# Attention with beacon keys into a two-layer network: transposes moved from TensorE to DMA from the third batch on, and the first two batches reordered

## The chip, the cores and the metric

The kernel runs on one core of a Trainium2 chip. The metric is device time in microseconds (us), as the median of several runs of the whole program. A profile is one more execution, recorded by the hardware profiler; its span is the time from its first instruction to its last.

The core has five engines, each with its own queue of instructions that it takes in order: TensorE (PE in the profile; PEld is its weight load), VectorE (DVE), ScalarE (ACT), GpSimd (POOL) and SyncE (SP). SP does no arithmetic here: it issues DMAs. ScalarE and GpSimd issue DMAs as well, between their other work. An instruction that has to wait stops everything behind it in its engine's queue.

## The reference

Eight batches, eight heads, 576 queries and keys of width 64, and 16 extra "beacon" keys per head that every query sees:

```python
k_all = np.concatenate([beacon_k, k], axis=2)
v_all = np.concatenate([beacon_v, v], axis=2)
scores = scale * np.matmul(q, k_all.transpose(0, 1, 3, 2))
causal = np.zeros((S, Nb + S), dtype=bool)
causal[:, Nb:] = np.triu(np.ones((S, S), dtype=bool), k=1)
scores = np.where(causal, -1000000000.0, scores)
a = np.exp(scores - scores.max(-1, keepdims=True))
a /= a.sum(-1, keepdims=True) + 1e-09
attn_out = np.matmul(a, v_all)
x = attn_out.transpose(0, 2, 1, 3).reshape(B * S, H * D)   # 4608 x 512
h = x @ w_in                                               # 512 x 2048
out = np.maximum(0.01 * h, h) @ w_out                      # 2048 x 512
```

## The kernel before, in words

**Pairs and steps.** Attention is done by pairs of heads, numbered g = 0 to 31; a batch b has four pairs, hp = 0 to 3, so g = 4b + hp. The loop at the end of the kernel runs over g; I call one turn of it a step. A pair passes through three steps: in step g its scores and exponentials, in step g + 2 its values (`value`, two halves), in step g + 3 its output is transposed into `xT` (`finish`). The program order within each engine is the order in which the code writes the instructions (`manual_schedule`).

**Q and K.** `load_qk` (L137) loads two pairs of a batch (a "group", grp 0 or 1) by DMAs that GpSimd issues, into `q_raw` and `k_raw`. `permute` (L167), on GpSimd apart from the first tiles, copies them into `q_nat` and `k_nat`, 128 partitions by 9 blocks of 128. `t_q` (L229 to L252) transposes one pair: nine TensorE transposes of 64x128 into PSUM (tag `tp`), for Q and again for K, and a copy by VectorE into `qT` or `kT` that also puts the rows into order (L249). The transposed beacon keys (`bkT`) are copied into the first 16 columns of `kT` (L239).

**Scores and values.** `score(g, n)`, n = 0 to 3, multiplies into one of two PSUM buffers (pool `ps_sc`), and ScalarE takes the exponential out of it into `aT` (L278, L282). `masks` (L292 to L305, VectorE) zeroes the upper triangles. `value` multiplies `aT` with the values (tile `av` in PSUM); VectorE takes the reciprocal of the sums and writes `x_nat` (L342, L343). `x_transposes` (L355) transposes `x_nat` with five TensorE transposes, and VectorE copies into `xT` (L360).

**V.** `load_v` (L211, L214, L216) loads a batch's values by six DMAs that SP issues; `cast_v` (L225) turns them to bf16, on VectorE for batches 0 and 1, on GpSimd after that. The load of batch 2 (in `loads(3)`) is tied with `behind` to the last load of `w_out`, so that it starts only when the weights are there.

**The network as filler.** The second part is cut into 9 chunks of 512 tokens. `moe1` (L369) is four matmuls and a ScalarE activation into `gT` (L376); `moe2` (L385) is four matmuls, and after every fourth call a VectorE copy into `osb` (L394) and a store that SP issues (L396). `fill()` puts one of these calls where the step has a `slot`: none in steps 0 to 5, four in steps 6 and 7, eight from step 9 on, and a longer hand-written row of them in step 8, which also empties batch 1. A chunk can be filled only when `finish` of the last pair of its batch has raised `ready`.

**PSUM.** All of `tp`, `av` and `acc` (the filler's accumulator) take turns in one pool of four buffers, `ps_one`: the fifth tile waits until the first is read out.

**Loads in the loop.** `loads(g)` stands at the head of each step. For batches 1 to 6 it starts the next batch: values and Q/K loads at hp 0 and 1, `permute` at hp 2 and 3, `cast_v` at hp 3.

Of the kernel before, what the change touches and what calls it, by code (L numbers as in the profile page):

```python
# [15 lines left out]
def kernel(  # L16
# [24 lines left out]
    RI = 9  # L41
# [25 lines left out]

    singles = ctx.enter_context(tc.tile_pool(name="singles", bufs=1))
    rawpool = ctx.enter_context(tc.tile_pool(name="rawpool", bufs=2))
    qkpool = ctx.enter_context(tc.tile_pool(name="qkpool", bufs=4))  # L70
    natpool = ctx.enter_context(tc.tile_pool(name="natpool", bufs=3))
    headpool = ctx.enter_context(tc.tile_pool(name="headpool", bufs=2))
    gpool = ctx.enter_context(tc.tile_pool(name="gpool", bufs=2))
    opool = ctx.enter_context(tc.tile_pool(name="opool", bufs=3))
# [129 lines left out]
            reason="loads in order of need",  # L204
        )

    def load_v(b, after=None):

        t = rawpool.tile([128, NKB, H, D], FP32, name="v_raw")
        v_raws[b] = t  # L210
        first = nc.sync.dma_start(out=t[0:NB, 0], in_=beacon_v[b].rearrange("h p d -> p h d"))  # L211
        if after is not None:
            behind(first, after)
        nc.sync.dma_start(out=t[NB:128, 0], in_=v[b, :, 0:112].rearrange("h p d -> p h d"))  # L214
        for c in (1, 2, 3, 4):
            last = nc.sync.dma_start(  # L216
                out=t[0 : ROWS[c], c],
                in_=v[b, :, OFF[c] : OFF[c] + ROWS[c]].rearrange("h p d -> p h d"),
            )
        return last  # L220
# [8 lines left out]
    def t_q(g, which, copy=nc.vector.tensor_copy):  # L229

        b, hp = divmod(g, NPAIR)
        grp, e = divmod(hp, 2)
        ps_ = slice(e * RP, (e + 1) * RP)
        if which == 0:
            dst = headpool.tile([128, S], BF16, name="qT")
            qk[g] = [dst]
        else:
            kT = headpool.tile([128, NB + S], BF16, name="kT")
            nc.vector.tensor_copy(out=kT[:, 0:NB], in_=bkT[:, b, hp])  # L239
            qk[g].append(kT)  # L240
            dst = kT[:, NB : NB + S]
        ps = ps_one.tile([128, 1024], BF16, name="tp", tag="one")
        for i in range(RI):
            nc.tensor.transpose(  # L244
                ps[:, i * RP : (i + 1) * RP],
                nat[b, grp][which][ps_, i].rearrange("p h d -> p (h d)"),
                ident[ps_, ps_],
            )
        copy(  # L249
            out=dst.rearrange("c (p i) -> c p i", i=RI),  # L250
            in_=ps[:, 0:S].rearrange("c (i p) -> c p i", i=RI),
        )  # L252

    probs = {}

# [58 lines left out]
    def value(g, half):  # L314
        b, hp = divmod(g, NPAIR)
        aT = probs[g]
        va = v_bufs[b % 2]
        if half == 0:
            xs[g] = (
                headpool.tile([128, 5, 2, D], BF16, name="x_nat"),  # L320
                headpool.tile([128, 10], FP32, name="rec"),
            )
        x_nat, rec = xs[g]
        t0, t1 = ((0, 3), (3, 5))[half]
        av = ps_one.tile([128, 512], FP32, name="av", tag="one")
        avv = av[:, 0 : (t1 - t0) * 132].rearrange("p (n w) -> p n w", w=66)
        for t in range(t0, t1):
            q0, _ = QT[t]
            for par in range(2):
                n = (t - t0) * 2 + par  # L330
                for c in range(t + 1):
                    a0 = acol(c, q0)
                    nc.tensor.matmul(  # L333
                        out=avv[:, n, 0 : D + 1],
                        lhsT=aT[0 : ROWS[c], par, a0 : a0 + 128],
                        rhs=va[0 : ROWS[c], c, 2 * hp + par, :],
                        start=(c == 0),
                        stop=(c == t),
                        skip_group_check=True,
                    )  # L340
        n0, n1 = t0 * 2, t1 * 2
        nc.vector.reciprocal(out=rec[:, n0:n1], in_=avv[:, :, D])  # L342
        nc.vector.tensor_tensor(  # L343
            out=x_nat[:, t0:t1].rearrange("p t e d -> p (t e) d"),
            in0=avv[:, :, 0:D],
            in1=rec[:, n0:n1, None].to_broadcast([128, n1 - n0, D]),
            op=ALU.mult,
        )

    def x_transposes(g):  # L350
        b, hp = divmod(g, NPAIR)
        x_nat, _ = xs.pop(g)
        ps = ps_one.tile([128, 1024], BF16, name="tp", tag="one")
        for t, (q0, rows) in enumerate(QT):
            nc.tensor.transpose(  # L355
                ps[:, q0 : q0 + rows],
                x_nat[0:rows, t].rearrange("p e d -> p (e d)"),
                ident[0:rows, 0:rows],
            )
        nc.vector.tensor_copy(out=xT[:, hp, b * S : (b + 1) * S], in_=ps[:, 0:S])  # L360

    gT = {}

# [71 lines left out]
    with order:  # L435
# [24 lines left out]
        def loads(g):  # L460
            b, hp = divmod(g, NPAIR)
            if g == 1:
                for which in range(2):
                    permute(1, 0, which, nc.gpsimd.tensor_copy)
            elif g == 3:
                for which in range(2):
                    permute(1, 1, which, nc.gpsimd.tensor_copy)
                behind(load_w_in(0), v1)
                for i in range(1, 4):
                    load_w_in(i)  # L470
                for i in range(4):
                    w = load_w_out(i)
                load_v(2, after=w)
                load_qk(2, 0)
                load_qk(2, 1)
            elif b >= 1 and b < B - 1:
                if b > 1:
                    if hp == 0:
                        load_v(b + 1)
                    if hp < 2:  # L480
                        load_qk(b + 1, hp)
                if hp >= 2:
                    for which in range(2):
                        permute(b + 1, hp - 2, which, nc.gpsimd.tensor_copy)
                if hp == 3:
                    cast_v(b + 1, nc.gpsimd)

        def finish(g):

            x_transposes(g)  # L490
            b, hp = divmod(g, NPAIR)
            if hp == NPAIR - 1:
                ready[0] = NCH if b == B - 1 else b + 1


        for g in range(NG + 3):
            if has(g):
                loads(g)
            slots = [0] * 8 if g < 6 else [0, 0, 1, 1, 0, 1, 1, 0] if g < 8 else [1] * 8

            def slot(n):
                if slots[n]:
                    fill()

            if g == 2 * NPAIR:

                finish(g - 3)
                value(g - 2, 0)
                fill()
                value(g - 2, 1)  # L510
                fill()
                value(g - 1, 0)
                finish(g - 2)
                value(g - 1, 1)
                fill()
                fill()
                finish(g - 1)
                for n in range(16):
                    fill()
                t_q(g, 0)  # L520
                t_q(g, 1)
                fill()
                fill()
                score(g, 0)
                score(g, 1)
                fill()
                fill()
                fill()
                t_q(g + 1, 0)
                t_q(g + 1, 1)  # L530
                score(g, 2)
                score(g, 3)
                fill()
                fill()
                masks(g)
                fill()
                continue

            late = g - 2 == 2 * NPAIR - 1 or g - 2 == 2 * NPAIR - 2
            if has(g):  # L540
                score(g, 0)
                score(g, 1)
            slot(0)
            if g == 2:
                cast_v(0, nc.vector)
            if g == NPAIR + 1:
                cast_v(1, nc.vector)
            if has(g - 3) and not 2 * NPAIR < g <= 2 * NPAIR + 2:
                finish(g - 3)
            slot(1)  # L550
            if has(g - 2) and not late:
                value(g - 2, 0)
            slot(2)
            slot(3)
            if has(g + 1) and g + 1 != 2 * NPAIR:
                t_q(g + 1, 0)
                t_q(g + 1, 1)
            if has(g):
                score(g, 2)
                score(g, 3)  # L560
            slot(4)
            if has(g - 2) and not late:
                value(g - 2, 1)
            slot(5)
            if g == 2:
                beacon_transposes(1, B)
            slot(6)
            if has(g):
                masks(g)
            slot(7)  # L570
# [32 lines left out]
```

The softmax here doesn't subtract the row's maximum and nothing guards it: scores larger than these inputs give would overflow.

## Time and profile before

| | |
|---|---|
| median of 13 runs | 379.05 us (375.95 to 380.94) |
| the profiled execution | 380.18 us, its span 378.5 us |
| ScalarE busy | 195.5 us (52%) |
| VectorE busy | 173.6 us (46%) |
| GpSimd busy | 101.9 us (27%) |
| DMA traffic | 33.82 MB, mean 89 GB/s |
| score matmuls of pair 8 begin at | 77.98 us |

The first stage (steps 0 to 7, to about 55 us) has attention and hardly any filler, and its loads keep the DMA engines busy. The second stage is attention with the filler between; the last part, from about 312 us, is filler alone. "Idle before" in a line of the profile is the time that the engine stood still just ahead of these instructions, with what released it.

### The profile page before, as it was taken

What the parts mean: (1) busy time and instruction counts of PE and PEld (TensorE: products, weight loads), DVE (VectorE), ACT (ScalarE), POOL (GpSimd) and SP (SyncE); (2) the same over time, 40 slices, a digit from 0 to 9 for tenths busy, and PEclk for the clock granted to TensorE, in tenths of its full rate; (3) what the DMA queues carried; (4) which work ended last, traced back from release to release, by engine and by line L of the source; (5) the groups of instructions that cost most, each with busy time, mean ns of one, the idle gap of its engine ahead of it and who ended that gap; (6) DMA issues with size and microseconds to landing.
All of it is one profiled execution on the core that took longest, in us unless ns stands there. A gap on an engine that the chain in (4) does not pass through costs nothing.

```text
span 378.5 us, 7668 instructions
## 1 busy us (share of the span) xinstructions
PE 355.2 (94%) x3217; PEld 189.0 (50%) x3264; DVE 173.6 (46%) x402; ACT 195.5 (52%) x308; POOL 101.9 (27%) x143
## 2 busy tenths in 40 slices
PE   4878799999999899999999999999999999999996
PEld 3455455444555455545554555555555554444442
DVE  2669763063556664564456545644455233000021
ACT  3936585366536785347634873377336801643310
POOL 8479126657202822082018202300000000000000
PEclk9999899999999999999999999999999999999999
DMA  8898999946319930169014901100010002001012
GB/s 169 152 211 139 202 204 201 199 105 113 69 57 203 183 54 2 57 119 189 4 56 83 225 7 50 44 21 2 28 57 29 1 29 83 2 0 57 28 55 83
DMA packets 58370, 33.82 MB, mean 89 GB/s; under 512 B 41440, under 2 KB 53472, under 8 KB 58336
## 3 DMA queue, kind: packets, MB, share of 16 engines
q0 software_dynamic: 13152, 13.34, 22.5%
q1 hardware_dynamic: 44896, 19.67, 20.8%
q8 instruction: 25, 0.41, 0.4%
q10 hardware_dynamic: 288, 0.33, 0.3%
q14 instruction: 9, 0.07, 0.1%
HBM read 37.22 MB, written 9.44 MB: 123 GB/s over the span
## 4 chain that ended last, share of the span: by engine, by line
PE 84%; DVE 8%; DMA 3%; POOL 2%; issue 1%; SPq 1%; ACT 0%
PE acc L385 33%; PE acc L369 32%; PE av L333 7%; PE sc L267 6%; PE tp L244 4%; PE tp L355 2%; DMA v_raw<-in_v_dram 1%; DMA v_raw<-in_k_dram 1%; DVE osb L394 1%; DVE xT L360 1%; DVE x_nat L343 1%; SPq L216 1%; DVE qT L249 1%; DVE kT L249 1%; POOL k_raw L137 1%
## 5 line engine op out<-in xcount | busy, mean ns | idle before, releaser
L278 ACT ACTIVATE aT<-sc 128x928 bf16<-128x928 f32 (+2 forms) x128 | 102.5, 855 | 78.1 <-PE sc L267 77.9
L369 PE MATMUL acc<-xT,w_in_sb 128*128 128x512 bf16 x551 | 138.2, 380 | 3.6 <-DVE xT L360 2.1
L385 PE MATMUL acc<-w_out_sb,gT 128*128 128x512 bf16 x554 | 135.6, 379 | 1.5 <-issue 0.6
L376 ACT ACTIVATE gT<-acc 128x512 bf16<-128x512 f32 x144 | 85.6, 600 | 82.2 <-PE acc L369 81.0
L369 PEld LDWEIGHTS <-w_in_sb 128*128 128x128 bf16 x576 | 52.6, 98 | 60.0 <-issue 5.1
L385 PEld LDWEIGHTS <-gT 128*128 128x128 bf16 x576 | 52.1, 98 | 60.0 <-issue 5.3
L394 DVE COPY osb<-acc 128x512 f32<-128x512 f32 x36 | 24.8, 690 | 93.5 <-PE acc L385 93.0
L267 PE MATMUL sc<-qT,kT 64*128 64x128 bf16 (+5 forms) x384 | 43.1, 313 | 6.7 <-DVE kT L249 3.5
L333 PEld LDWEIGHTS <-aT 128*128 128x128 bf16 (+1 forms) x960 | 39.3, 101 | 16.4 <-issue 3.0
L333 PE MATMUL av<-v_aug,aT 128*128 128x65 bf16 (+1 forms) x960 | 42.5, 198 | 1.0 <-DVE xT L360 0.6
L167 POOL COPY q_nat<-q_raw 128x1152 bf16<-128x1152 bf16 (+1 forms) x16 | 18.3, 1145 | 85.7 <-PE tp L244 57.5
L249 DVE COPY qT<-tp 128x576 bf16<-128x576 bf16 x32 | 24.2, 755 | 34.4 <-PE tp L244 34.4
L343 DVE TENSOR_TENSOR x_nat<-av,rec 128x384 bf16<-128x384 f32 x64 | 31.4, 491 | 2.2
L267 PEld LDWEIGHTS <-kT 64*128 64x128 bf16 (+1 forms) x384 | 18.5, 101 | 20.9 <-issue 11.5
L225 POOL CAST v_aug<-v_raw 128x512 bf16<-128x512 f32 (+1 forms) x30 | 19.3, 683 | 33.2 <-PE av L333 31.5
L360 DVE COPY xT<-tp 128x576 bf16<-128x576 bf16 x32 | 14.5, 453 | 29.8 <-PE tp L355 29.8
L342 DVE RECIPROCAL rec<-av 128x6 f32<-128x6 f32 x64 | 11.9, 185 | 33.6 <-PE av L333 33.6
L137 POOL DMA_DIRECT2D k_raw<-in_k_dram x31 | 20.8, 671 | 9.8 <-DMA w_out_sb<-in_moe_w_out_dram 5.0
L249 DVE COPY kT<-tp 128x576 bf16<-128x576 bf16 x31 | 23.2, 748 | 0.0
L137 POOL DMA_DIRECT2D q_raw<-in_q_dram x31 | 19.5, 629 | 11.7 <-DMA v_raw<-in_v_dram 5.1
L299 DVE TENSOR_TENSOR aT<-aT,mask 128x768 bf16<-128x768 bf16 x32 | 21.6, 675 | 1.2 <-ACT aT L278 1.2
L167 POOL COPY k_nat<-k_raw 128x1152 bf16<-128x1152 bf16 (+1 forms) x16 | 18.7, 1171 | 0.6 <-DMA k_raw<-in_k_dram 0.6
(33 smaller groups left out, 150.3 us busy)
## 6 DMA issues: line engine op xcount, KB each, us to landing
out_dram<-osb SPq DMA_DIRECT2D x36, 256.0 KB, 2.0
v_raw<-in_v_dram SPq DMA_DIRECT2D x24, 256.0 KB, 6.0
q_raw<-in_q_dram POOLq DMA_DIRECT2D x31, 144.0 KB, 6.2
k_raw<-in_k_dram POOLq DMA_DIRECT2D x31, 144.0 KB, 6.5
w_in_sb<-in_moe_w_in_dram POOLq DMA_DIRECT2D x4, 512.0 KB, 8.1
w_out_sb<-in_moe_w_out_dram POOLq DMA_DIRECT2D x4, 512.0 KB, 16.7
v_raw<-in_v_dram SPq DMA_DIRECT2D x8, 224.0 KB, 4.8
v_raw<-in_v_dram SPq DMA_DIRECT2D x8, 160.0 KB, 5.3
```

Source lines behind the costliest of these rows:

```text
L137: dma = nc.gpsimd.dma_start(out=dst[e * RP : (e + 1) * RP], in_=src[b, h0 : h0 + 2].rearrange("h (p i) d -> p h i d", i=RI),)
L167: copy(out=dst[p0:p1], in_=src[p0:p1].rearrange("p h i d -> p i h d"))
L249: copy(out=dst.rearrange("c (p i) -> c p i", i=RI), in_=ps[:, 0:S].rearrange("c (i p) -> c p i", i=RI),)
L267: nc.tensor.matmul(out=sc[0 : ROWS[c], par, col - c0 : col - c0 + w], lhsT=kT[ps_, c * 128 : c * 128 + ROWS[c]], rhs=qT[ps_, q0 : q0 + w], ...
L278: last = nc.scalar.activation(out=aT[:, :, c0 : c0 + w], in_=sc[:, :, 0:w], func=AF.Exp, scale=0.125)
L299: nc.vector.tensor_tensor(out=diag, in0=diag, in1=tri[:, None, None, :].to_broadcast([128, 2, 3, 128]), op=ALU.mult,)
L333: nc.tensor.matmul(out=avv[:, n, 0 : D + 1], lhsT=aT[0 : ROWS[c], par, a0 : a0 + 128], rhs=va[0 : ROWS[c], c, 2 * hp + par, :], start=(c = ...
L343: nc.vector.tensor_tensor(out=x_nat[:, t0:t1].rearrange("p t e d -> p (t e) d"), in0=avv[:, :, 0:D], in1=rec[:, n0:n1, None].to_broadcast( ...
L369: nc.tensor.matmul(out=acc, lhsT=w_in_sb[:, j, fc * 128 : (fc + 1) * 128], rhs=xT[:, j, i * 512 : (i + 1) * 512], start=(j == 0), stop=(j ...
L376: nc.scalar.activation(out=gT[i][:, fc, :], in_=acc, func=AF.Prelu, alpha=0.01)
L385: nc.tensor.matmul(out=acc, lhsT=gT[i][:, fc, t * 128 : (t + 1) * 128], rhs=w_out_sb[:, fc, :], start=(fc == 0), stop=(fc == NF - 1),)
L394: nc.vector.tensor_copy(out=osb, in_=acc)
```

## The change

Two things are changed, and buffers with them.

First, steps 0 to 7 get an order of their own: the transposes of the next pair stand between the first two and the last two scores; in odd steps ScalarE copies K's transposes out of PSUM instead of VectorE; `finish` comes at the end of the step; the beacon keys' transposes and the two casts on VectorE move to other steps.

Second, from batch 2 on, Q and K are transposed by DMA (`turn_pairs`, two DMAs for a group of two pairs, issued by SP) and then put into order by VectorE from SBUF (`in_order`), a step ahead of use. The output of the first three pairs of each batch is transposed by DMA as well (`x_turn`, three DMAs issued by SP); the last pair of each batch keeps the TensorE transposes. The loads of the values of batches 3 to 7 are issued by ScalarE; that of batch 2 stays on SP. Step 8 has two `fill()` fewer.

```diff
-    qkpool = ctx.enter_context(tc.tile_pool(name="qkpool", bufs=4))
-    natpool = ctx.enter_context(tc.tile_pool(name="natpool", bufs=3))
+    qkpool = ctx.enter_context(tc.tile_pool(name="qkpool", bufs=3))
+    natpool = ctx.enter_context(tc.tile_pool(name="natpool", bufs=2))
+    turnpool = ctx.enter_context(tc.tile_pool(name="turnpool", bufs=2))
...
-    def load_v(b, after=None):
+    def load_v(b, after=None, queue=nc.sync):
...
+    turned = {}
+
+    def turn_pairs(b, grp):
+
+        tiles = []
+        for which, name in enumerate(("q_turn", "k_turn")):
+            t = turnpool.tile([128, RI, 2, RP], BF16, name=name)
+            nc.sync.dma_start_transpose(
+                out=t.rearrange("c i e p -> c i (e p)"),
+                in_=nat[b, grp][which].rearrange("r i h d -> r (i h d)"),
+            )
+            tiles.append(t)
+        turned[b, grp] = tiles
+
+    def in_order(g, eng):
+
+        b, hp = divmod(g, NPAIR)
+        grp, e = divmod(hp, 2)
+        qT = headpool.tile([128, S], BF16, name="qT")
+        kT = headpool.tile([128, NB + S], BF16, name="kT")
+        eng.tensor_copy(out=kT[:, 0:NB], in_=bkT[:, b, hp])
+        for t, dst in zip(turned[b, grp], (qT, kT[:, NB : NB + S])):
+            eng.tensor_copy(
+                out=dst.rearrange("c (p i) -> c p i", i=RI),
+                in_=t[:, :, e].rearrange("c i p -> c p i"),
+            )
+        qk[g] = [qT, kT]
...
-                headpool.tile([128, 5, 2, D], BF16, name="x_nat"),
+                headpool.tile([128, 5, 2, D], BF16, name="x_nat", bufs=3),
...
+    def x_turn(g):
+
+        b, hp = divmod(g, NPAIR)
+        x_nat, _ = xs.pop(g)
+        flat = x_nat.rearrange("p t e d -> p t (e d)")
+        dst = xT[:, hp, b * S : (b + 1) * S]
+        nc.sync.dma_start_transpose(out=dst[:, None, 0:112], in_=flat[0:112, 0])
+        nc.sync.dma_start_transpose(
+            out=dst[:, 112:496].rearrange("p (t q) -> p t q", t=3),
+            in_=flat[:, 1:4].rearrange("p t x -> p (t x)"),
+        )
+        nc.sync.dma_start_transpose(out=dst[:, None, 448:576], in_=flat[:, 4])
...
                 if b > 1:
                     if hp == 0:
-                        load_v(b + 1)
+                        load_v(b + 1, queue=nc.scalar)
                     if hp < 2:
                         load_qk(b + 1, hp)
                 if hp >= 2:
                     for which in range(2):
                         permute(b + 1, hp - 2, which, nc.gpsimd.tensor_copy)
+                    turn_pairs(b + 1, hp - 2)
                 if hp == 3:
                     cast_v(b + 1, nc.gpsimd)
+            if g + 1 >= 2 * NPAIR and has(g + 1):
+                in_order(g + 1, nc.vector)
 
         def finish(g):
 
-            x_transposes(g)
             b, hp = divmod(g, NPAIR)
+            if b < 2 or hp == NPAIR - 1:
+                x_transposes(g)
+            else:
+                x_turn(g)
...
                 for n in range(16):
                     fill()
-                t_q(g, 0)
-                t_q(g, 1)
-                fill()
-                fill()
                 score(g, 0)
                 score(g, 1)
                 fill()
                 fill()
                 fill()
-                t_q(g + 1, 0)
-                t_q(g + 1, 1)
                 score(g, 2)
                 score(g, 3)
...
+            if g < 2 * NPAIR:
+
+                score(g, 0)
+                score(g, 1)
+                if g == 3:
+                    beacon_transposes(1, B)
+                if g + 1 < 2 * NPAIR:
+                    t_q(g + 1, 0)
+                    t_q(g + 1, 1, nc.scalar.copy if g % 2 else nc.vector.tensor_copy)
+                slot(2)
+                if g != 2 and has(g - 2):
+                    value(g - 2, 0)
+                slot(3)
+                score(g, 2)
+                score(g, 3)
+                if g == 2:
+                    cast_v(0, nc.vector)
+                    value(0, 0)
+                slot(5)
+                if has(g - 2):
+                    value(g - 2, 1)
+                slot(6)
+                if g == NPAIR:
+                    cast_v(1, nc.vector)
+                if has(g - 3):
+                    finish(g - 3)
+                masks(g)
                 continue
```

The old places of `beacon_transposes(1, B)`, of the two casts and of `t_q(g + 1, ...)` in the general step are taken out. Steps from 9 on are otherwise as before.

More of the change, by code (lines that the diff above doesn't have):

```diff
@@ L205, in behind @@
         )
-    def load_v(b, after=None):
+    def load_v(b, after=None, queue=nc.sync):
         t = rawpool.tile([128, NKB, H, D], FP32, name="v_raw")
         v_raws[b] = t
-        first = nc.sync.dma_start(out=t[0:NB, 0], in_=beacon_v[b].rearrange("h p d -> p h d"))
+        first = queue.dma_start(out=t[0:NB, 0], in_=beacon_v[b].rearrange("h p d -> p h d"))
         if after is not None:
             behind(first, after)
-        nc.sync.dma_start(out=t[NB:128, 0], in_=v[b, :, 0:112].rearrange("h p d -> p h d"))
+        queue.dma_start(out=t[NB:128, 0], in_=v[b, :, 0:112].rearrange("h p d -> p h d"))
         for c in (1, 2, 3, 4):
-            last = nc.sync.dma_start(
+            last = queue.dma_start(
                 out=t[0 : ROWS[c], c],
@@ L537 @@
                 continue
+            if g < 2 * NPAIR:
[24 more added lines that the diff above has]
+                masks(g)
+                continue
             late = g - 2 == 2 * NPAIR - 1 or g - 2 == 2 * NPAIR - 2
@@ L543 @@
             slot(0)
[L544 to L547, printed above, removed]
             if has(g - 3) and not 2 * NPAIR < g <= 2 * NPAIR + 2:
@@ L554 @@
             slot(3)
-            if has(g + 1) and g + 1 != 2 * NPAIR:
-                t_q(g + 1, 0)
-                t_q(g + 1, 1)
             if has(g):
@@ L564 @@
             slot(5)
-            if g == 2:
-                beacon_transposes(1, B)
             slot(6)
```

## The prediction, made before the changed kernel was run

> **What bounds the kernel now.** I read the page's busy table first, then the timeline of TensorE in a steady group, then the timelines and waits of the engines that the change loads: SP's queue, ScalarE, VectorE.
>
> ```profile
> PE 355.2 (94%) x3217; PEld 189.0 (50%) x3264; DVE 173.6 (46%) x402; ACT 195.5 (52%) x308; POOL 101.9 (27%) x143
> ```
>
> TensorE is busy for 94% of 378.5 us. The timeline of TensorE in pair 19's and 20's steps (start us, length us, engine, line, tiles, count; lengths overlap, so cost is read from start to start):
>
> ```profile
> 174.98 0.44 PE L355 MATMUL tp<-ident,x_nat 112*128 112x112 bf16 x5
> 175.25 1.03 PE L369 MATMUL acc<-xT,w_in_sb 128*128 128x512 bf16 x4
> ...
> 178.31 0.43 PE L244 MATMUL tp<-ident,q_nat 64*128 64x64 bf16 x9
> 178.58 0.36 PE L244 MATMUL tp<-ident,k_nat 64*128 64x64 bf16 x7
> ...
> 178.84 0.50 PE L267 MATMUL sc<-qT,kT 64*128 64x336 bf16 x7
> ...
> 188.12 0.43 PE L244 MATMUL tp<-ident,q_nat 64*128 64x64 bf16 x9
> ```
>
> A step repeats every 9.81 us (178.31 to 188.12) with no idle. The 18 Q/K transposes take 0.53 us (178.31 to 178.84; below I use 0.52), the five of the attention output 0.27 us (174.98 to 175.25), a fill of four matmuls 0.864 us. So in the second stage whatever leaves TensorE is time saved, and whatever holds TensorE is time lost.
>
> SP's queue in the first stage, by the timeline, and its longest wait, by the view of waits:
>
> ```profile
> 21.20 1.08 SPq L216 DMA_DIRECT2D v_raw<-in_v_dram  x1
> 56.29 0.33 SPq L211 DMA_DIRECT2D v_raw<-in_beacon_v_dram  x1
> 56.67 0.43 SPq L214 DMA_DIRECT2D v_raw<-in_v_dram  x1
> 57.14 6.26 SPq L216 DMA_DIRECT2D v_raw<-in_v_dram  x4
> ```
> ```profile
> SPq L211 <- DMA w_out_sb<-in_moe_w_out_dram: 33.9, 1, 33.9
> ```
>
> After batch 1's values SP stands still for 33.9 us: the load of batch 2's values is tied behind the last piece of `w_out`. It issues from 56.29 to 63.40. Nothing behind it in SP's queue can start before 63.4; before the change that is nothing urgent.
>
> ScalarE in step 20, by its timeline (first line: the last `moe1` activation of step 19):
>
> ```profile
> 183.50 0.60 ACT L376 ACTIVATE gT<-acc 128x512 bf16<-128x512 f32 x1 [0.27 <-PE acc L369]
> 183.99 1.86 ACT L278 ACTIVATE aT<-sc 128x1024 bf16<-128x1024 f32 x2
> 185.72 0.62 ACT L376 ACTIVATE gT<-acc 128x512 bf16<-128x512 f32 x1
> 189.05 1.35 ACT L278 ACTIVATE aT<-sc 128x928 bf16<-128x928 f32 x2 [2.71 <-PE sc L267]
> ```
>
> ScalarE has slack over the step, but its two exponentials come at once at the start, and scores 2 and 3 (about 188.5) need their two PSUM buffers.
>
> **What the Trainium skill says.** "DMA: Bandwidth & Descriptors", section "Anatomy of one DMA", says that a DMA's semaphore wait happens on the issuing sequencer before dispatch: SP's 33.9 us above agree. Its section "Issuing engines are not separate DMA queues" says that another issuing engine saves only sequencer time: so values on ScalarE cost ScalarE what they cost SP. "VectorE: DVE Perf Modes", section "The three transpose paths", prices a 128x128 bf16 transpose by DMA at 1.309 us; "Advanced Engine Details and Errata", section "X-Bar Transpose (TRN2)", expects 350 to 400 GB/s. No run shown has a DMA transpose.
>
> **The change part by part.**
>
> *TensorE work removed.* Pairs 8 to 31 lose 18 transposes each: 24 x 0.52 = 12.5 us. Pairs of batches 2 to 7 other than each batch's last lose the output's: 18 x 0.27 = 4.9 us. All of it is on the path.
>
> *VectorE.* The copies into qT and kT stay (0.755 and 0.748 us before, from PSUM); from SBUF with a strided source I take 0.7 each (0.6 to 0.8), and 18 xT copies of 0.453 go. At 46% busy neither matters; where they stand does.
>
> *The wait added at step 7.* `loads(7)` now puts `in_order(8)` at the head of VectorE's step 7. It reads the tiles of `turn_pairs(2, 0)`, which stands in SP's queue behind the values of batch 2, so it issues at 63.4 at the earliest (POOL's copies into q_nat and k_nat end at 60.0 and are no later). Two DMA transposes of 128x1152 bf16, 295 KB each: at 350 GB/s, with the 2.0 us that an output store takes from issue to landing as a floor, the first lands in 2.8 us; at nine times 1.309 us, in 11.8. I take 6 us for both (bounds 4 and 24), as 1152 pieces of 256 B each at the 28 ns that a packet of q1 takes (20.8% of 16 x 378.5 us over 44896), 2.0 us by 16 engines, plus the 2.0 us floor, plus 2.0 for the second. They land at 69.4; kT copy 0.7 and reciprocal and product 0.75 follow: 70.9.
> Behind `in_order(8)` on VectorE wait the outputs of pair 5, the xT copy of pair 4 and the masks of pair 7. TensorE runs on until `ps_one` is full: step 7 allocates acc, av, acc, acc, av, acc over four buffers, and the last (slot 6) needs the buffer of the av that VectorE has not emptied. Before, that slot began at 54.6 (53.75 plus one fill of 0.864); now at 70.9. When step 7 itself starts (45 or so) doesn't matter, the release is set by SP. Cost +16.3, and 1.5 for slow matmuls after the stop (the trace shows this after the 1.38 us gap at 41.78: four scores 0.94 instead of 0.59, twelve values 0.87 instead of 0.53, seven fill matmuls 2.20 instead of 1.67, five transposes 0.70 instead of 0.45, less overlap about 1.4).
>
> *The reordering of the first two batches* (transposes earlier, half the kT copies on ScalarE at 0.64 us, values behind scores) aims at the 3.5 us that scores wait for kT. It is worth -3.5 to +1 by itself and 0 here, because step 7's stop absorbs it. It costs fills: `finish(3)` moves to the end of step 6, so step 6 has none, and with slot 6 late three are done at the stop instead of seven. These four and the two that step 8 drops refill the starved steps 12 to 14.
>
> *Values on ScalarE.* `load_v(b+1)` at hp 0 now holds ScalarE for six issues: 0.38 + 0.45 + 4.6 to 4.9 (114.06 to 119.5) is 5.5 us, more where other loads run (11.16 for four at 167.06). In steps 16, 20 and 24 it comes between the last `moe1` activation (ends 0.7 us into the step) and the two exponentials, which end at 7.2 and 8.1 us; scores 2 and 3 are due at 4.3. TensorE waits 2.9 and 0.6, 3.5 us, and runs slow after it, 1.3: 3 x 4.8 = 14.4. In step 12 the fills before it are `moe2` only, ScalarE is early, nothing. In step 8 the second fill's buffer is needed 3.3 us on and freed at about 6.5 to 9: 4 us. Bounds: 0 if issuing doesn't hold ScalarE; 44 if each of the four loads meets traffic as at 167.06 (12.0 us for six issues in place of 5.5). I take 4 + 14.4 = 18.4.
>
> *Queues later on.* In later batches `turn_pairs` reaches SP in mid-step 4b+1 (after the third output store), 14 us before `in_order` wants it; `x_turn` has a step or more, also with its third transpose waiting for the overlapping second. The pools that shrink (qkpool 4 to 3, natpool 3 to 2) cost nothing: from batch 2 on a q_nat tile is free once its transposing DMA has read it, where before it waited for TensorE (POOL's waits of 16 us on L244). All of this holds while a pair of transposes takes under 9 us.
>
> *The sum, against the span 378.5:* slot 6 +16.3; slow clock +1.5; step 8: two fills and t_q(8) fewer, the transposes of pair 4 more, -1.73 -0.63 +0.27 = -2.1; ScalarE there +4.0; t_q(9) to t_q(12) and one output -2.4; steps 12 to 14, with six more fills (+5.2), 1.6 of Q/K and 0.5 of output transposes less, and 1.4 of the idle 2.5 us used, +1.7; steps 15 on, 16 x 0.52 and 15 x 0.27, -12.4; ScalarE +14.4. Together +21.0: 399.5. The profiled execution took 380.18, 1.7 over its span and 1.1 over the median of 379.05. So 401.2 by its own measure, 400 against the median.
>
> **Rivals.**
> 1. *Issuing on ScalarE hides* (its queue runs beside the compute): 400 - 18.4 = 381.6. For it: at 0.84 to 1.96 two issues run beside ScalarE's table load. Against: POOL's copies stand behind its issues.
> 2. *The wait at step 7 is covered*: the faster side. If the turned tiles are there by about 49, slot 6 starts at about 50.5 (45.5, plus 5.0 us of scores, values and fills), 20.4 sooner, and the 1.5 go too: 400 - 21.9 = 378 with ScalarE held, 360 with rival 1 as well, which is the case I give the chance to. Each us of landing after 49 costs a us, so its gain is gone at 68. For it: from step 8 on nothing that the change adds on SP is late. Against: SP would have to be clear some 19 us sooner.
> 3. *DMA transposes take 1.309 us per block of 128x128*, the skill's higher price: step 7's release moves 18 us to 88, and each batch has 36 + 15 blocks, 67 us against a batch of 36. The DMA side bounds: six batches at 67 behind 63, over 450.
>
> **How the numbers follow.** Forecast 0.66 at 400 (its own range 386 to 413: transposes +-3 us, ScalarE 6 to 31, two loads in traffic), rival 1 0.12, rival 2 0.12, rival 3 0.10. The range 381 to 416 holds the first two and leaves about 0.2 out. A measurement here tells 0.5% (1.9 us) from no change; half of rival 1 is within it. Faster 0.12, same 0.06, slower 0.82.
>
> **What would show it.** A VectorE wait of some 20 us in step 7, ended by a DMA onto q_turn or k_turn, with TensorE idle from about 50 to 70; turn_pairs issued right after the values of batch 2; then steps of 9.0 us in place of 9.8 except steps 16, 20 and 24, where TensorE waits about 3 us for ScalarE at scores 2. The prediction is wrong if that transpose is issued before 60, or if ScalarE's exponentials don't move when it issues loads.

## The result and the profile after

The changed kernel took 409.93 us (median of 11 runs, 405.34 to 412.49) against 379.09 us before: a ratio of 1.078 (95% interval 1.074 to 1.081), slower by 30.8 us. The ratios leave out executions more than 1.5% above the fastest of their kernel; over the others the changed kernel's median is 407.74 us, and what an edit gains is counted from there. The forecast was 400, with a range of 381 to 416. The profiled execution took 407.52 us, its span is 405.8 us.

The busy table of the page (busy us, share of the span, instructions):

```profile
PE 344.9 (85%) x2699; PEld 173.7 (43%) x2742; DVE 155.8 (38%) x381; ACT 195.5 (48%) x311; POOL 108.4 (27%) x143
```

TensorE is busy for 10.3 us less than before in a span that is 27.3 us longer: work went away, and more waiting came. The timeline of TensorE shows the largest piece (start us, length us, engine, line, tiles, count; in brackets the idle time before and what ended it):

```profile
49.21 1.03 PE L411 MATMUL acc<-xT,w_in_sb 128*128 128x512 bf16 x3
50.07 0.44 PE L384 MATMUL tp<-ident,x_nat 112*128 112x112 bf16 x5
73.89 0.94 PE L384 MATMUL tp<-ident,x_nat 112*128 112x112 bf16 x5 [23.37 <-DVE x_nat L372]
```

TensorE stands still from 50.5 to 73.9 us. `x_nat`, which it waits for, is VectorE's, and VectorE's timeline says why it is late:

```profile
46.37 0.16 DVE L275 COPY kT<-bkT 128x16 bf16<-128x16 bf16 x1
69.93 0.64 DVE L277 COPY qT<-q_turn 128x576 bf16<-128x576 bf16 x1 [23.40 <-DMA q_turn<-q_nat]
72.48 0.65 DVE L277 COPY kT<-k_turn 128x576 bf16<-128x576 bf16 x1 [1.91 <-DMA k_turn<-k_nat]
73.05 0.19 DVE L371 RECIPROCAL rec<-av 128x6 f32<-128x6 f32 x1
```

The copies of `in_order(8)` stand in front of the reciprocal at 73.05, which needs nothing from them. SP's queue by the timeline:

```profile
55.54 0.44 SPq L215 DMA_DIRECT2D v_raw<-in_v_dram  x1
56.02 8.68 SPq L217 DMA_DIRECT2D v_raw<-in_v_dram  x4
64.81 1.95 SPq L262 DMA_TRANSPOSE q_turn<-q_nat  x1
66.86 2.04 SPq L262 DMA_TRANSPOSE k_turn<-k_nat  x1
```

The transposing DMAs are issued directly after the values of batch 2, which had waited 30.1 us for `w_out`.

Where TensorE has no stop the change does what it removes. A late pair of steps:

```profile
179.54 0.59 PE L296 MATMUL sc<-qT,kT 64*128 64x512 bf16 x4
180.06 1.90 PE L427 MATMUL acc<-w_out_sb,gT 128*128 128x512 bf16 x8
...
188.55 0.59 PE L296 MATMUL sc<-qT,kT 64*128 64x512 bf16 x4
```

From score to score that is 9.01 us, where it was 9.81. But every fourth step is long. ScalarE in step 24 (ACTq lines are DMAs that it issues):

```profile
248.34 0.60 ACT L418 ACTIVATE gT<-acc 128x512 bf16<-128x512 f32 x1 [0.27 <-PE acc L411]
248.43 0.34 ACTq L212 DMA_DIRECT2D v_raw<-in_beacon_v_dram  x1
249.08 1.25 ACTq L215 DMA_DIRECT2D v_raw<-in_v_dram  x1
250.37 6.39 ACTq L217 DMA_DIRECT2D v_raw<-in_v_dram  x4
256.86 1.86 ACT L307 ACTIVATE aT<-sc 128x1024 bf16<-128x1024 f32 x2 [7.92 <-DMA xT<-x_nat]
```

and TensorE beside it:

```profile
257.94 0.57 PE L296 MATMUL sc<-qT,kT 64*128 64x336 bf16 x4 [5.19 <-ACT aT L307]
```

The exponentials of scores 0 and 1 start about 8 us late, and TensorE waits 5.19 us for a score buffer. The step takes 16.86 us (248.24 to 265.10). Steps 12, 16 and 20 take 13.51, 11.48 and 13.30.

Where the time went, by the starts of scores in the two traces:

| stretch | before | after | difference | forecast |
|---|---|---|---|---|
| start to score of pair 8 | 77.98 | 96.31 | +18.3 | +19.7 |
| pair 8 to pair 12 | 34.84 | 32.47 | -2.4 | -2.4 |
| pair 12 to pair 16 | 30.94 | 39.28 | +8.3 | +0.9 |
| pair 16 to the last `finish` | 174.96 | 177.88 | +2.9 | +2.8 |
| filler alone at the end | 59.7 | 59.9 | +0.1 | 0 |

The forecast's terms are those of its sum; its +1.7 and 0.8 of the -12.4 fall into the third row, the rest of the -12.4 and the 14.4 into the fourth.

### The profile page after: what moved, and what is told of

Read it like the earlier page. It is cut to its first block, busy times and chain, and to the rows that moved or that the text cites. A ratio compares the mean times of both kernels' runs of the same rounds, so it can differ in the third digit from the quotient of the medians.

```text
span 405.8 us, 6779 instructions
## 1 busy us (share of the span) xinstructions
PE 344.9 (85%) x2699; PEld 173.7 (43%) x2742; DVE 155.8 (38%) x381; ACT 195.5 (48%) x311; POOL 108.4 (27%) x143
## 4 chain that ended last, share of the span: by engine, by line
PE 67%; DMA 12%; DVE 4%; SPq 2%; ACT 2%; POOL 2%; ACTq 2%; issue 1%; another core or an unknown queue 1%
PE acc L411 29%; PE acc L427 27%; PE av L362 6%; PE sc L296 5%; DMA w_out_sb<-in_moe_w_out_dram 5%; DMA xT<-x_nat 3%; ACT aT L307 2%; DMA v_raw<-in_v_dram 1%; DMA k_turn<-k_nat 1%; ACTq L217 1%; DMA out_dram<-osb 1%; SPq L217 1%; DVE osb L436 1%; POOL w_in_sb L112 1%
## 5 line engine op out<-in xcount | busy, mean ns | idle before, releaser
L427 PE MATMUL acc<-w_out_sb,gT 128*128 128x512 bf16 x554 | 137.7, 387 | 2.1 <-issue 1.6
L296 PE MATMUL sc<-qT,kT 64*128 64x128 bf16 (+5 forms) x384 | 41.1, 309 | 18.0 <-ACT aT L307 15.5
L362 PEld LDWEIGHTS <-aT 128*128 128x128 bf16 (+1 forms) x960 | 42.0, 104 | 21.2 <-issue 8.0
L226 POOL CAST v_aug<-v_raw 128x512 bf16<-128x512 f32 (+1 forms) x30 | 23.8, 831 | 90.2 <-PE av L362 88.0
L362 PE MATMUL av<-v_aug,aT 128*128 128x65 bf16 (+1 forms) x960 | 45.2, 204 | 2.4 <-DVE v_aug L226 1.9
L168 POOL COPY q_nat<-q_raw 128x1152 bf16<-128x1152 bf16 (+1 forms) x16 | 20.4, 1278 | 54.2 <-DMA q_raw<-in_q_dram 30.2
L296 PEld LDWEIGHTS <-kT 64*128 64x128 bf16 (+1 forms) x384 | 15.4, 101 | 44.3 <-issue 38.9
L384 PE MATMUL tp<-ident,x_nat 128*128 128x128 bf16 (+1 forms) x70 | 6.9, 232 | 23.7 <-DVE x_nat L372 23.4
L277 DVE COPY qT<-q_turn 128x576 bf16<-128x576 bf16 x24 | 15.4, 643 | 23.4 <-DMA q_turn<-q_nat 23.4
L277 DVE COPY kT<-k_turn 128x576 bf16<-128x576 bf16 x24 | 15.5, 644 | 1.9 <-DMA k_turn<-k_nat 1.9
```

The costliest lines, as they stand in the source:

```text
L168: copy(out=dst[p0:p1], in_=src[p0:p1].rearrange("p h i d -> p i h d"))
L226: eng.tensor_copy(out=dst[0 : ROWS[c], c, :, 0:D], in_=t[0 : ROWS[c], c])
L277: eng.tensor_copy(out=dst.rearrange("c (p i) -> c p i", i=RI), in_=t[:, :, e].rearrange("c i p -> c p i"),)
L296: nc.tensor.matmul(out=sc[0 : ROWS[c], par, col - c0 : col - c0 + w], lhsT=kT[ps_, c * 128 : c * 128 + ROWS[c]], rhs=qT[ps_, q0 : q0 + w], ...
L362: nc.tensor.matmul(out=avv[:, n, 0 : D + 1], lhsT=aT[0 : ROWS[c], par, a0 : a0 + 128], rhs=va[0 : ROWS[c], c, 2 * hp + par, :], start=(c = ...
L427: nc.tensor.matmul(out=acc, lhsT=gT[i][:, fc, t * 128 : (t + 1) * 128], rhs=w_out_sb[:, fc, :], start=(fc == 0), stop=(fc == NF - 1),)
```

## The experiments

All kernels below start from the changed kernel unless said otherwise. Each ratio is to the kernel before.

### The wait at step 7 alone

`in_order(8)` and `in_order(9)` are moved to step 8, directly ahead of the score of pair 8.

```diff
-            if g + 1 >= 2 * NPAIR and has(g + 1):
+            if g + 1 > 2 * NPAIR + 1 and has(g + 1):
                 in_order(g + 1, nc.vector)
...
                 for n in range(16):
                     fill()
+                in_order(g, nc.vector)
+                in_order(g + 1, nc.vector)
                 score(g, 0)
```

> The changed kernel with in_order(8) and in_order(9) moved from the heads of steps 7 and 8 to just before the first scores of pair 8. Own theory (two separate waits, and in step 8 the second stands behind the first): VectorE is free, but ScalarE has already taken up the load of batch 3's values at about 50.5 and, as in the changed kernel's trace, comes free only at about 70; TensorE then stops some four fills into step 8 on the activations and goes on at about 70.5. The time falls by only 2 to 6 us, to 404 to 408. Rival A (VectorE's wait is the whole of the stop): the stop of 23.4 us goes, 385 to 389. Rival B (the stop only reflects late DMA data of batch 2, wherever it is awaited): same as the changed kernel within 2 us, with the wait now just before the scores of pair 8.

Measured: 400.35 us, ratio 1.056 (1.052 to 1.060). The place of the stop was the expected one; the time lies below the 404 to 408 of my theory. VectorE no longer stops TensorE, but TensorE stops all the same, 4.8 us later (at 55.3 us in place of 50.5). TensorE's timeline, and then ScalarE's:

```profile
70.43 0.68 PE L384 MATMUL tp<-ident,x_nat 112*128 112x112 bf16 x5 [15.13 <-ACT gT L418]
```

```profile
48.97 0.45 ACTq L215 DMA_DIRECT2D v_raw<-in_v_dram  x1
63.10 6.63 ACTq L217 DMA_DIRECT2D v_raw<-in_v_dram  x4
69.78 2.06 ACT L418 ACTIVATE gT<-acc 128x512 bf16<-128x512 f32 x4 [20.82 <-DMA q_turn<-q_nat]
```

ScalarE has issued two loads of batch 3's values and stands before the third for 14 us, though the two before it went into the same buffer without a wait. The view puts its final release down to a transposing DMA of SP. ScalarE's wait for SP lay hidden under VectorE's. The gain is 7.9 us (399.84 in the executions that the ratio counts) and not the full 23, because the second wait takes over. The traced execution took 406.66, the longest of the four. It reaches pair 8 8.3 us earlier than the changed kernel's (88.05 against 96.31), but its steps 16 and 20 are 3.1 and 4.1 us longer: there the exponentials wait 5.97 and 8.35 us, where the changed kernel's wait 4.49 and 4.69.

### The values' issue alone

All values are issued by SP again; `in_order` stays where the change put it.

```diff
-                        load_v(b + 1, queue=nc.scalar)
+                        load_v(b + 1)
```

> The changed kernel with the values of all batches issued by SP again (VectorE's order unchanged). Own theory: steps 12, 16, 20 and 24 lose their excess over 9.0 us (4.5, 2.5, 4.3 and 7.9 us in the trace), the stop in step 7 stays (about 23 us): 19 us less, 389 to 393. Rival A (issuing on ScalarE costs nothing, the excess of these steps has another cause such as DMA traffic): within 3 us of 410. Rival C (SP is then late with the turned tiles, VectorE waits for them in each batch): slower than 410.

Measured: 399.65 us, ratio 1.057 (1.053 to 1.061). The long steps 12, 16, 20 and 24 are gone, and the stop at step 7 stays, with 21.68 us. But only 8.1 us came back, where I had expected 19. SP now reaches the transposing DMAs that step 15 needs later, and they take longer to issue beside the Q and K loads of GpSimd (2.9, 6.9 and 6.4 us where 1.3 is usual). TensorE there:

```profile
163.29 1.17 PE L362 MATMUL av<-v_aug,aT 128*128 128x65 bf16 x18 [6.79 <-DVE x_nat L372]
164.27 5.21 PE L411 MATMUL acc<-xT,w_in_sb 128*128 128x512 bf16 x12
```

VectorE had stood 9.62 us before its copy from `q_turn`. It is the wait of step 7 once more, two batches on. The twelve fill matmuls after it take 5.21 us, where twelve take 2.75 without a stop.

### Both waits removed

Both edits together.

> Both edits together. Own theory: neither stop is left, only the gains on TensorE and up to 3 us of wait for the turned tiles of batch 2 (there at about 72, wanted at about 71): 364 to 370, faster than the kernel before by 3 to 4%. Rival A (ScalarE costs nothing): like the run with only VectorE's edit, 385 to 389. Rival C (the DMA side can't carry it): 379 or more.

Measured: 370.12 us in the profiled execution, and 381.34, 381.84 and 382.66 us in three others, for which no ratio can be given; none is quite inside the 364 to 370 of my theory. The same kernel was run once more to see what the longer executions have that the shorter has not.

> The kernel with both edits once more, for a second trace: its times were 370.1 once and 381 to 383 three times. Own theory: in the longer executions the turned tiles of batch 4 come later still, VectorE's waits for q_turn and k_turn in step 15 are longer by about 11 us. Rival: the excess lies in steps of other batches, or in the matmul times.

Measured: 379.44 us. My expectation named the wrong place. TensorE stops in step 14, and waits for the attention output's transposing DMA (`x_turn`), which writes `xT`:

```profile
121.87 0.61 PE L411 MATMUL acc<-xT,w_in_sb 128*128 128x512 bf16 x1 [3.19 <-DMA xT<-x_nat]
133.79 1.01 PE L411 MATMUL acc<-xT,w_in_sb 128*128 128x512 bf16 x2 [11.31 <-DMA xT<-x_nat]
```

In the shorter execution the largest wait of that region is 3.68 us. The piece of `x_turn` that ends the long wait was issued at 125.63, after GpSimd had begun to issue eight Q and K loads (122.0), and landed 8.1 us later, at 133.75. In the shorter execution the same piece was issued at 119.3, before these loads (121.4), and took 2.4 us. So with the two waits gone a third comes up, and it comes up in some executions only: what differs between these two traces is whether the piece goes ahead of the loads, and no run set that order on purpose.

### The first part alone

The kernel before, with the reordering of the first two batches and nothing else.

```diff
+            if g < 2 * NPAIR:
+
+                score(g, 0)
+                score(g, 1)
...
+                masks(g)
+                continue
```

> The kernel before with only the first part of the change (steps 0 to 7 in the new order, half the K copies on ScalarE), all transposes on TensorE. In the changed kernel step 7 ends at 50.5 with four fills done, before at 55.5 with eight, which is 1.5 us for the reordering. Own theory: 375 to 378.5 against 379, since four fills move into steps 12 and 13, which were short of them. Rival: the fills lost in step 6 cost their full 3.5 us, 380 to 383.

Measured: 375.84 us (375.40 to 376.81), ratio 0.992 (0.990 to 0.995). The first part gains 3.0 us by itself (378.89 before, beside it), as expected. All of the loss is the second part's.

### The transposing DMAs a step earlier

From the version with both waits removed; the copies and the DMAs for the next batch start at hp 1 and 2.

```diff
-                if hp >= 2:
+                if 1 <= hp <= 2:
                     for which in range(2):
-                        permute(b + 1, hp - 2, which, nc.gpsimd.tensor_copy)
-                    turn_pairs(b + 1, hp - 2)
+                        permute(b + 1, hp - 1, which, nc.gpsimd.tensor_copy)
...
+            if 1 <= b < B - 1 and 1 <= hp <= 2:
+                turn_pairs(b + 1, hp - 1)
```

> The kernel with both edits (in_order(8) late, values on SP), and the permutes and DMA transposes of a batch a step earlier (hp 1 and 2 in place of 2 and 3). Both edits alone ran between 370 and 383; its trace shows VectorE waiting 5 us for k_turn in step 15, because step 13 is short and SP's transposes then stretch to 5 us each beside the loads. Own theory (the remaining loss is that lateness): the wait in step 15 goes, 362 to 368, and the runs lie closer together. Rival (DMA side is full there, whatever the order): as before, 370 to 383, with the wait elsewhere.

Measured: 376.06 us (372.92 to 383.23), ratio 0.990 (0.981 to 0.999), hardly better than before; the 362 to 368 that I expected was missed. Q and K are now early, and the output's transposes are what is late:

```profile
134.46 1.03 PE L411 MATMUL acc<-xT,w_in_sb 128*128 128x512 bf16 x2 [15.34 <-DMA xT<-x_nat]
```

### The values on GpSimd, with and without the output's transposes by DMA

`in_order` late as in the first experiment, all values from batch 2 on issued by GpSimd, and those of batch 2 no longer tied to `w_out`. The second kernel is the same with `x_transposes` for every pair.

```diff
-            if b < 2 or hp == NPAIR - 1:
-                x_transposes(g)
-            else:
-                x_turn(g)
+            x_transposes(g)
```

> The kernel with in_order(8) late and all values from batch 2 on issued by GpSimd, batch 2's behind its Q/K loads and not tied to w_out. Own theory: SP is clear for the turned tiles of batch 2 when q_nat is there (60), they land by 66, no wait at step 8; no load holds ScalarE or SP: 360 to 367. Rival (GpSimd becomes late: six more issues a batch before its permutes and casts): 370 to 380, with VectorE or TensorE waiting for v_aug or q_turn.

> As the run with values on GpSimd, but all outputs transposed by TensorE again (no x_turn). Own theory (the term of 18 x 0.27 = 4.9 us is right, SP's third-transpose waits cost nothing): 4 to 6 us slower than the run with values on GpSimd. Rival (the transposes of the output by DMA crowd SP and the DMA engines, and cost more than they save): equal or faster.

Measured: with `x_turn` 367.45 to 391.4 us over 19 runs, median 380.08, too scattered for a ratio, and not the 360 to 367 of my theory; in the profiled one (374.94) TensorE waits 9.60 us, once, behind a copy from `k_turn`. Without it 367.50 us (367.15 to 368.76), ratio 0.971 (0.965 to 0.977). My theory expected the second to be slower by the 4.9 us of TensorE work; the rival was right. Taking 18 output transposes off TensorE costs more than it saves, and brings the scatter.

### The output's transposes by TensorE, in the changed kernel and with the values on SP

The same edit of `x_turn`, once in the changed kernel with both waits left in, and once in the version with both waits removed and the values on SP.

> The changed kernel with one thing undone: every pair's attention output is transposed on TensorE, as before the change; both waits (step 7, and ScalarE issuing the values) stay. My theory: within the changed kernel the output's transposing DMAs cost little directly (TensorE's wait of 2.0 us in step 14) and something through ScalarE (in step 24 it waits 7.9 us for such a DMA, and TensorE 3 us more than in steps 16 and 20), and undoing them gives 4.9 us back to TensorE: 402 to 410 us, with TensorE idle for about 23 us in step 7 and for 1.8 to 2.2 us at scores 2 of steps 12, 16, 20 and also 24. Rival: they cost as much here as in the version with the values on GpSimd, where undoing them took the median from 380 to 367.5: 390 to 399 us.

> The version with both waits removed (all values issued by SP, in_order late), and every output transposed on TensorE. My theory: the output's transposing DMAs are what made that version range from 370 to 383 us; without them it stands at 365 to 370 us with all runs within 1%, whoever issues the values, and no TensorE wait above 3 us follows a transposing DMA. Rival: the values on SP, in front of the transposing DMAs of Q and K, are what holds it; then 373 to 383 us, with TensorE waiting 4 to 10 us in step 15 for k_turn.

Measured: 402.54 us (ratio 1.062, 1.058 to 1.066) and 367.49 us (366.57 to 368.64; ratio 0.968, 0.965 to 0.972).

The second shows that it doesn't matter whether SP or GpSimd issues the values once `x_turn` is gone: SP (367.49) and GpSimd (367.50) give the same time. Against the version with `x_turn` and values on SP, the spread of runs falls from 12.5 us to 2.1. The largest TensorE wait between 75 and 260 us in that kernel is this one, which no DMA ends:

```profile
121.37 0.59 PE L411 MATMUL acc<-xT,w_in_sb 128*128 128x512 bf16 x1 [2.04 <-DVE xT L389]
```

The first lands just inside my theory's range. `x_turn` cost the changed kernel 5.2 us (402.54 against 407.74), although it took 4.9 us of work from TensorE. In the two spans the difference is 6.3 us. Without `x_turn` step 12 is 4.2 us shorter and step 24 3.4. Step 14 is 1.6 shorter, but TensorE waits the same 2.0 us there in both, for a copy that VectorE makes; what differs is the clock granted after it (0.64 and 1.00), and that is not shown to be `x_turn`'s doing: the version with the values on SP has 0.64 there too, without `x_turn`. Another 1.0 us lies ahead of pair 8, and most other steps are 0.3 longer without `x_turn`. ScalarE in step 12 of this kernel shows how it costs:

```profile
124.19 0.34 ACTq L212 DMA_DIRECT2D v_raw<-in_beacon_v_dram  x1
124.56 1.61 ACTq L215 DMA_DIRECT2D v_raw<-in_v_dram  x1
...
126.22 3.60 ACTq L217 DMA_DIRECT2D v_raw<-in_v_dram  x4
129.92 1.02 ACT L307 ACTIVATE aT<-sc 128x1024 bf16<-128x1024 f32 x1 [4.40 <-DMA v_raw<-in_v_dram]
```

The issue holds ScalarE for 4.40 us instead of 8.13, and TensorE doesn't wait in step 12 at all. In steps 16, 20 and 24 its waits at scores 2 are 1.27, 1.93 and 1.97 us, where they were 1.76, 1.95 and 5.19; so the part of my expectation that put step 16 at 1.8 us or more, and a wait in step 12, was off.

## Why the prediction was right, point by point

**The wait at step 7** was right in place, mechanism and nearly in size. The chain is the one forecast: `w_out`, values of batch 2, `turn_pairs(2, 0)`, VectorE, TensorE. Issue was forecast for 63.4 and came at 64.81; both landings for 69.4 and came by 72.5; TensorE's release for 70.9, and it came at 73.89. Of these 3.0 us, 1.4 are the later issue; the rest is that each DMA landed 5.1 and 5.6 us after its own issue, where the forecast had 4.0 for the first and the second 2.0 behind it. One link failed: TensorE did not stop for a PSUM buffer at slot 6, which still found one (49.21), but for data. The output transposes at the head of step 8 need the `x_nat` of pair 5, which VectorE had not written. In the compiled program slot 6 takes a buffer that ScalarE had emptied: the buffers of `ps_one` do not go strictly in turn, as I had said of them. Up to pair 8 the sum was only 1.4 us too high, and that is luck in part: the release came 3.0 late, and the +4 of step 8 did not show.

**Values on ScalarE.** In steps 16, 20 and 24 the forecast was 14.4 us; the excesses over 9.0 us are 2.5, 4.3 and 7.9, 14.7 together. The sum was good, the single values were not: they range from half to over 1.5 times the 4.8 that each was given. That the sum fits is luck in part: in the kernel without `x_turn`, where a step is 9.28 us, the three excesses are 2.0, 4.3 and 4.2, 10.5 together, and the long step 24 comes from a coupling that the forecast did not have (below). *Step 12 at nothing* was the term that failed. It cost 4.5 us. The forecast's reason, that ScalarE is early there because the fills before are `moe2` only, holds for a hold of 4.4 us, as the kernel without `x_turn` shows. The hold was 8.13 us. *Step 8 at +4* was not seen, because it lies under the stop of step 7; the first experiment showed it as a wait of 15 us.

**What stretches ScalarE's hold.** The forecast priced six issues by their own durations and by traffic. The traces show another cause. In the compiled program the DMAs of SP and ScalarE share eight completion counters in turn, and a DMA waits until the earlier user of its counter has landed. The list of instructions has the wait beside the load, here the third load in step 8 and the sixth in step 24:

```
50 L217 DMACopy v_raw<-in_v_dram 128x8x64 [waits DMAHW1_49]
...
175 L217 DMACopy v_raw<-in_v_dram 80x8x64 [waits DMAHW0_49]
```

The earlier users are SP's second load of batch 2's values and a first piece of `x_turn`. The landings agree with the issues: SP's load at 55.54 landed after 8.6 us, at 64.12, and ScalarE's third load was issued at 64.14. The piece of `x_turn` that SP issued at 250.82 landed after 5.6 us, at 256.4, and ScalarE's sixth load was issued at 256.4. In step 12 the sixth load went out at 133.94, when an output store of 128.80 had landed after 5.1 us, at 133.92; that store stood in SP's queue behind a piece of `x_turn`. The Trainium skill, "DMA: Bandwidth & Descriptors", section "Anatomy of one DMA", says, in its account of a DMA that GpSimd issues, that a semaphore wait is made on the issuing sequencer before dispatch. The three landings agree, and it would explain why exponentials stand behind it. No run gave ScalarE's loads counters of their own, so how much of each hold is this wait and how much is the loads' own issue is known only where a landing fits.

**`x_turn` at nothing.** This is the other term that failed. The forecast said that `xT` has a step or more. In the changed kernel it cost through ScalarE, 4.2 us in step 12 and 3.4 in step 24, and not by being late itself: no wait of TensorE there ends with it. With the two waits gone it was late itself, by 11 to 15 us around step 14, where the filler waits for the batch that has just been finished. What it asks of SP shows in the view of SP's waits of the changed kernel (us in total, times, longest):

```profile
SPq L402 <- DMA xT<-x_nat: 42.3, 18, 6.0
```

The third piece overlaps the second and waits for it, 18 times, and everything behind it in SP's queue waits too.

**The third row of the table**, 7.4 us over its forecast, is mostly these two terms: 4.5 us are step 12. Another 1.6 are the slower matmuls after the wait of 2.04 us in step 14. About 1.2 is idle time that the forecast wanted to fill: TensorE's stops in steps 13 and 14 took 2.3 us before and still take 2.0.

**Work removed.** 0.52 us a pair for Q and K and 0.27 for an output were right: 9.01 us a step instead of 9.81. Pairs 8 to 12 gave -2.37 us for a forecast of -2.4, and pair 16 to the end +2.9 for +2.8.

**The price of a transposing DMA.** The forecast took 6 us for the first pair, between 4 and 24. From the first issue to the second landing it took 7.7. Over the run one lands 3.5 us after issue in the median, and up to 14.4. That speaks against counting the Trainium skill's 1.309 us for a 128x128 block ("VectorE: DVE Perf Modes", section "The three transpose paths") once for each block of a larger transpose, which would give 11.8 us for nine blocks. It also speaks against taking as the price of one DMA the 350 to 400 GB/s that the prediction quotes: 295 KB in 3.5 us from issue to landing is 84 GB/s. Rival 3 is out.

**Rivals.** Rival 1 (the issue hides) fell in steps 12 to 24. Rival 2 (wait covered) didn't happen; made to happen, it gives 370 to 383 us and not the 360 that the forecast had for it, since `x_turn` then sets the time.

**The loss as a whole.** The forecast was right in direction and range, but 9.9 us short of the median. Between the two profiles it is 6.3 short: +7.4 in the third row, -1.4 up to pair 8 and 0.3 in the others. The rest comes from which executions were profiled: the one before was 1.1 us over its median, this one 2.4 under. The two waits and `x_turn` taken out together give 367.5, 40.3 us less than 407.74. The edits don't add up singly: 7.9 for the first wait, 8.1 for the second, 5.2 for `x_turn`, because each one taken out uncovers another. What is left of the change, the reordering and Q and K by DMA, gains 11.8 us on the kernel before. The reordering has 3.0 of it. Q and K have the other 8.8, where 12.5 us of TensorE work go away. The difference lies ahead of pair 16: its scores begin at 139.2 us with the transposes of eight pairs gone, and at 139.0 with the reordering alone. By pair 4, before any turned tile is used, 1.6 us are lost, TensorE waits 1.1 us for `kT` at pair 8, and step 14 takes 12.67 us against 10.36; why pair 4 is later was not traced.

## What to carry to other kernels

When a step is moved to another queue, list what stands in front of it there at its first use, and not only in the steady state: here steady steps gained 0.8 us each and the first one lost 23. A copy that needs a late transfer should stand at the last place in its engine's order where its result is still in time, because everything behind it waits. And when the bounding wait has been found, take it out and look again before pricing the gain: here a second wait lay under the first and a third came up behind them, and the last came from a transpose that was cheaper on the busiest engine than off it.

## What the runs showed that I had not expected

- In the compiled program DMAs of different issuing engines are coupled by shared completion counters: ScalarE stood before a load for 14 us (49.4 to 63.1 in the first experiment) until an unrelated load of SP had landed (63.08).
- A transposing DMA's issue isn't of fixed length. For Q and K it holds SP for 1.33 and 1.44 us in the median, and up to 6.0 us in the changed kernel, 6.9 with values on the same queue and 7.6 in the version without `x_turn`.
- The same stop of TensorE slows what follows in one execution and not in another. In step 14 it waits 2.04 us in the changed kernel, 2.03 in that kernel without `x_turn` and 2.04 in the version with all values on SP and without `x_turn`, each time for the same copy into `xT`. The clock granted in the 3 to 5 us after it was 0.64, 1.00 and 0.64. So in these traces the length of the stop alone does not decide it.
